# Carrying the softmax normalisation of five attention units through DRAM instead of TensorE

## The chip, the cores and the metric

The kernel runs on one core of one Trainium2 chip. The metric is the device time of one execution in microseconds (us); lower is better. The core has a matrix engine (TensorE, "PE" in the rows), a vector engine (VectorE, "DVE"), an activation engine (ScalarE, "ACT"), GpSimd ("POOL") and SyncE ("SP"), which here only starts DMA transfers. Each engine works through its own list of instructions in order. Between engines, an instruction waits on semaphores that others raise.

## The reference

Three stages follow one another. Only the first matters for the change.

```python
def _attn_ref(q, k, v):                       # batch 2, 8 heads, 576 positions, head size 64
    scores = scale * np.matmul(q, k.transpose(0, 1, 3, 2))
    ...                                       # bias by distance, window of 128 keys, causal
    attn = np.exp(scores - np.max(scores, axis=-1, keepdims=True))
    attn = attn / (np.sum(attn, axis=-1, keepdims=True) + 1e-09)
    return np.matmul(attn, v)

def reference(**kwargs):
    x = _attn_ref(...)                        # 1152 tokens x 512
    x = _moe_ref(x, ...)                      # 4 experts, 512 -> 1024 -> 512, relu, weighted sum
    return _moe2_ref(x, ...)                  # 512 -> 2048, h*cos(h), -> 512
```

## The kernel before, in words

**Attention.** The queries are cut into nine units of 128 columns. They are worked in the order `units = [1, 2, 3, 4, 0, 5, 6, 7, 8]`; this text numbers the nine by their place, 0 to 8, so place 4 is unit 0 (the first 64 queries of both batches, with 64 keys each). A unit has eight heads, done as two groups of four, so the list `sched` has 18 entries, and the loop in `attention` has a step k for each, two steps to a unit. The entries of place i are 2i and 2i+1.

In step k the program writes these pieces in this order (each engine takes its own parts of them in the same order):

- `att_transpose` of entry k-2: TensorE turns the probabilities into a PSUM tile `t_ps` (L525); VectorE (L531) and ScalarE (L532) copy half each into `pt`.
- `att_scores` of entry k: TensorE makes scores (`s_ps`, L443/L448/L455); VectorE adds the bias and takes the extreme, four instructions a step (L468, "reductions" below); ScalarE takes the exponentials and their sums into `dens` (L474).
- `att_factors` of entry k-2, if it is the second of its unit: TensorE turns the broadcast reciprocal sums `wide` into a PSUM tile `r_ps`, four transposes (L499), and ScalarE copies them to `rs` (L503).
- `att_sums` of entry k-1, likewise: VectorE adds the sums and takes reciprocals (L486, L489), GpSimd broadcasts them to `wide` (L491).
- `fill(k)`: one piece of weight preparation on GpSimd, sometimes a product of the next stage on TensorE (`fills`: steps 12, 13, 15, 16), and then `stage()`, which advances the generators that normalise finished units.
- `att_pv` of entry k-3 up to step 9 and of entry k-2 from step 9 on (step 9 does both): TensorE multiplies by the values into the PSUM tile `x_ps` (L546/L561).

When both entries of a unit are through `att_pv`, a generator `rest()` is queued. Its first advance runs `normal`, the VectorE product of `x_ps` and `rs` (L571), which is also the last read of `x_ps` for places 0 to 4. Then ScalarE and VectorE split the result into two parts (`own_early`, L355 and L190), or `transform_early` makes sums of two units.

**PSUM.** `x_ps` tiles come from a pool of two banks in turn, so the tile of place i+2 uses the bank of place i, and its first `att_pv` cannot start until the `normal` of place i has read that bank.

**Loads.** At the top of each even step, SyncE starts the loads of the unit two places ahead (`qt`, `kt`) and of the values `vt` of the unit at work.

**After attention** (from about 65 us on) come the two feed-forward stages: large products on TensorE, 128x512 each.

Of the kernel before, what the change touches and what calls it, by code (L numbers as in the profile page):

```python
# [10 lines left out]
F32 = mybir.dt.float32  # L11
# [5 lines left out]
ALU = mybir.AluOpType  # L17
# [3 lines left out]
B, H, S, D = 2, 8, 576, 64  # L21
# [9 lines left out]
NP = NB // 128  # L31
ND = DM // 128
# [20 lines left out]
def tile_kernel(ctx, tc, qT, kT, v, probs, w_1, w_2, w_in, w_out, out):  # L53
    nc = tc.nc
# [3 lines left out]
    dram = pool("dram", bufs=1, space=DRAM)  # L58
# [18 lines left out]
    mkp = ap("mkp", bufs=1)  # L77
# [4 lines left out]
    stp = ap("stp", bufs=6)  # L82
# [279 lines left out]
    def own_early(t, x1):  # L362

        hi, lo = parts(t)
        hi(B11, x1[:, 0:2])
        hi(B21, x1[:, 2:4])
        lo(B21, x1[:, 2:4], nc.gpsimd)
        yield
        lo(B11, x1[:, 0:2], nc.vector)
# [52 lines left out]
    state, xps = {}, {}  # L422

    dens = mkp.tile([128, 2, H, 2], F32, name="dens")

    def att_scores(u, g):
        i = place(u)[1] if u else 0
# [51 lines left out]

    recs, late = {}, {}  # L480

    def att_sums(u, g):
        if g == 0:
            return
        rec = stp.tile([128, H], F32, name="rec", tag="rec")
        nc.vector.tensor_reduce(  # L486
            out=rec, in_=dens[:, units.index(u) % 2], axis=mybir.AxisListType.X, op=ALU.add
        )
        nc.vector.reciprocal(out=rec, in_=rec)  # L489
        wide = recs[u] = stp.tile([128, H, D], F32, name="wide", tag="wide", bufs=1)  # L490
        nc.gpsimd.tensor_copy(wide, rec.unsqueeze(2).to_broadcast([128, H, D]))  # L491

    def att_factors(u, g):
        if g == 0:
            return
        rec = recs.pop(u)
        rt = ps1.tile([128, ND, 128], F32, name="r_ps", tag="o_ps")
        for d in range(ND):
            nc.tensor.transpose(  # L499
                rt[:, d, :], rec[:, 2 * d : 2 * d + 2].rearrange("p h d -> p (h d)"), ident  # L500
            )
        rs = stp.tile([128, ND, 128], F32, name="rs", tag="rs", bufs=2)
        nc.scalar.activation(out=rs, in_=rt, func=AF.Copy)  # L503
        recs[u] = rs
# [30 lines left out]
    def att_pv(u, g):  # L535
# [3 lines left out]
        xt = xps[u]  # L539
# [27 lines left out]
        if g == 1:  # L567

            def normal(out):
                rs = recs.pop(u)  # L570
                nc.vector.tensor_tensor(out=out, in0=xt, in1=rs, op=ALU.mult)  # L571

            def rest():
                if u == 0:
                    x1 = txp.tile([128, ND, 128], F32, name="x1", tag="x1", bufs=1)
                    normal(x1)
                    split(x0, x1, nc.gpsimd)
                    return
                t = (u - 1) % NP
                x1 = xk[:, :, t * 128 : (t + 1) * 128]  # L580
                if u <= NP:
                    normal(x1)
                    yield from own_early(t, x1)
                else:
                    normal(xt)
                    late[u] = transform_early(t, x1, xt, u == units[-1])
                    one, two, three, second, four, five = late[u]
                    if u >= units[-2]:
                        return
                    one()  # L590
                    two()
                    yield
                    if u < units[-3]:
                        for piece in (three, second, four, five):
                            piece()

            xps.pop(u)
            staged.append(rest())
# [5 lines left out]
    def load_units_to(k):  # L604
        while nloaded[0] < min(k, len(units)):
            load_unit(units[nloaded[0]])
            nloaded[0] += 1

    def attention(fill, finale):
        n = len(sched)  # L610
        at = lambda k, what: what(*sched[k]) if 0 <= k < n else None
        for k in range(n):
            if k % 2 == 0:

                load_units_to(k // 2 + 3)
                load_values(sched[k][0])
            at(k - LAG, att_transpose)
            at(k, att_scores)
            if k == n - 1:
                break  # L620
            at(k - LAG, att_factors)
            at(k - 1, att_sums)
            fill(k)
            if k <= CATCH:
                at(k - LAG - 1, att_pv)
            if k >= CATCH:
                at(k - LAG, att_pv)
        finale(n, at)
# [471 lines left out]
    def whole(step):  # L1100
        for _ in step:
            pass
# [115 lines left out]
    with tc.manual_schedule():  # L1218

        warm = probs_t[2][:, 0, :256]  # L1220
        nc.vector.memset(warm, 0.0)
        nc.vector.memset(dens, 1e-9)
        for _ in range(WARM):
            nc.tensor.matmul(  # L1224
                ps1.tile([128, 512], F32, name="o_ps", tag="o_ps")[:, :256],
                warm[:, :128], warm, start=True, stop=True,
            )
        load_units_to(2)
        constants()
        early = {}  # L1230
# [3 lines left out]
        def opening(j, kind):  # L1234
            early[j] = pair(0, j, kind)
            return early[j]

        def leftover(end):
# [2 lines left out]
            return half(first[0], end)  # L1241

        fills = {
            12: lambda: opening(0, 3), 13: lambda: early[0],
            15: lambda: leftover(False), 16: lambda: leftover(True),
        }

# [144 lines left out]
```

## Time and profile before

| | |
|---|---|
| median of 3 runs | 621.19 us (621.17 to 621.64) |
| profiled execution: time | 622.03 us |
| profiled execution: span of the core | 620.0 us |
| TensorE busy | 613.9 us, 99% of the span |
| VectorE, ScalarE, GpSimd busy | 453.0, 321.5, 353.0 us |

The span is the time between the first and the last instruction of the profile; the execution's own time is 2.0 us longer. Busy time of TensorE is the union of its matmuls with modelled ends, so small gaps between short matmuls can hide in it; they are read from the starts of instructions instead.

### The profile page before, as it was taken

The page shows a single profiled execution, that of the slowest core. Times are in us where ns is not written, and L with a number is a line of the kernel's source. Part 1 is how long each engine was busy: PE and PEld are TensorE (multiplying, and loading weights), DVE is VectorE, ACT ScalarE, POOL GpSimd, SP SyncE. Part 2 cuts the span into 40 slices and gives each one's busy share as a digit, 9 for nine tenths or more (in the row PEclk, how much of TensorE's full clock was granted, in tenths as well). Part 3 has the DMA queues.
Part 4 walks back from the last instruction along what each step waited for, and adds up shares of the span by engine and source line. Part 5 has one row for each costly group of instructions (what it writes and reads, how often), then busy time and mean ns, then how long its engine had stood idle before and what let it go on. Part 6 is the DMA issues. An engine that isn't in the chain of part 4 may idle for free.

```text
span 620.0 us, 9378 instructions
## 1 busy us (share of the span) xinstructions
PE 613.9 (99%) x3348; PEld 503.4 (81%) x3348; DVE 453.0 (73%) x780; ACT 321.5 (52%) x674; POOL 353.0 (57%) x335
## 2 busy tenths in 40 slices
PE   8999999999999999999999999999999999999998
PEld 6777888888888888888888888888888888888886
DVE  6868899589789789699689655668664664664663
ACT  6988554444443453443443421455873773673660
POOL 4877586383383373473473471496569479379330
PEclk9999999999999999999999999999999999999999
DMA  9641236347447347337245227621102202202003
GB/s 261 169 148 46 85 132 197 76 136 213 127 130 237 108 124 243 109 109 246 71 135 171 67 82 211 183 68 36 34 2 68 69 1 68 69 0 69 17 1 135
DMA packets 51246, 69.05 MB, mean 111 GB/s; under 512 B 6912, under 2 KB 31488, under 8 KB 51200
## 3 DMA queue, kind: packets, MB, share of 16 engines
q1 hardware_dynamic: 50656, 68.06, 36.1%
q8 instruction: 26, 0.43, 0.3%
q10 hardware_dynamic: 544, 0.39, 0.2%
q14 instruction: 20, 0.16, 0.1%
HBM read 53.76 MB, written 14.68 MB: 110 GB/s over the span
## 4 chain that ended last, share of the span: by engine, by line
PE 94%; ACT 2%; DVE 2%; POOL 1%; issue 1%; ACTq 0%; POOLq 0%; DVEq 0%
PE o_ps L913 43%; PE o_ps L720 35%; PE o_ps L774 5%; PE o_ps L1027 4%; PE x_ps L561 2%; PE t_ps L525 1%; PE s_ps L455 1%; PE r_ps L499 1%; PE o_ps L1224 1%; PE o_ps L953 0%; ACT u L658 0%; ACT r L659 0%; POOL w1t L190 0%; DVE p L468 0%; ACT u L666 0%
## 5 line engine op out<-in xcount | busy, mean ns | idle before, releaser
L913 PE MATMUL o_ps<-w2t,hpair 128*128 128x512 f32 x1044 | 241.5, 389 | 0.0
L913 PEld LDWEIGHTS o_ps<-w2t,hpair 128*128 128x128 f32 x1044 | 195.7, 188 | 40.7
L720 PE MATMUL o_ps<-xs,w1t 128*128 128x512 f32 x720 | 168.8, 390 | 0.0
L720 PEld LDWEIGHTS o_ps<-xs,w1t 128*128 128x128 f32 x720 | 134.8, 188 | 28.6 <-issue 0.5
L190 POOL TENSOR_TENSOR w2t<-raw,w2t 128x512 fp32r<-128x512 f32 x48 | 63.4, 1337 | 73.6 <-ACT w2t L214 73.4
L190 POOL TENSOR_TENSOR w1t<-raw,w1t 128x512 fp32r<-128x512 f32 x48 | 64.4, 1358 | 62.0 <-ACT w1t L214 61.6
L190 POOL TENSOR_TENSOR w1t<-sm,w1t 128x512 fp32r<-128x512 f32 x48 | 63.8, 1346 | 31.3 <-ACT w1t L214 31.0
L190 POOL TENSOR_TENSOR hpair<-u,hpair 128x512 fp32r<-128x512 f32 x30 | 40.2, 1346 | 52.4 <-ACT hpair L678 52.4
L720 PE MATMUL o_ps<-xz,w1t 128*128 128x512 f32 x288 | 69.8, 390 | 0.1
L313 ACT ACTIVATE cr<-cr 128x512 f32<-128x512 f32 x32 | 21.7, 679 | 81.7 <-DVE ca L307 81.7
L720 PEld LDWEIGHTS o_ps<-xz,w1t 128*128 128x128 f32 x288 | 53.8, 188 | 11.8 <-DVE c L822 0.7
L697 DVE SCALAR_TENSOR_TENSOR hpair<-o_ps,hpair 128x512 fp32r<-128x512 f32 x47 | 32.3, 687 | 19.2 <-ACT hpair L706 19.2
L706 ACT ACTIVATE hpair<-o_ps 128x512 fp32r<-128x512 f32 x47 | 28.0, 596 | 33.7 <-DVE o_ps L822 33.6
L214 ACT ACTIVATE w1t<-sm 128x512 fp32r<-128x512 f32 x44 | 27.6, 630 | 32.5 <-POOL sm L190 32.3
L934 DVE SCALAR_TENSOR_TENSOR accpair<-o_ps,pr,accpair 128x512 f32<-128x512 f32 x48 | 34.8, 745 | 10.4 <-PE o_ps L913 10.4
L662 DVE SCALAR_TENSOR_TENSOR u<-r,u 128x512 f32<-128x512 f32 x36 | 28.1, 781 | 14.1 <-ACT r L659 14.1
L942 DVE TENSOR_TENSOR accpair<-o_ps,accpair 128x512 f32<-128x512 f32 x23 | 15.7, 689 | 27.7 <-PE o_ps L913 27.7
L774 PE MATMUL o_ps<-w1t,x 128*128 128x512 f32 x144 | 35.7, 391 | 0.0
L822 DVE TENSOR_TENSOR o_ps<-o_ps,u 128x512 f32<-128x512 f32 x48 | 33.1, 691 | 3.0 <-PE o_ps L720 2.8
L913 PE MATMUL o_ps<-w2t,h 128*128 128x512 f32 x144 | 34.8, 389 | 0.0
L316 DVE SCALAR_TENSOR_TENSOR co<-cr,ca 128x512 f32<-128x512 f32 x32 | 33.4, 1043 | 1.4 <-ACT cr L313 0.4
L474 ACT ACTIVATE p<-p,nmax 128x192 f32<-128x192 f32 (+1 forms) x72 | 31.0, 437 | 5.2 <-DVE nmax L468 5.1
(147 smaller groups left out, 894.1 us busy)
## 6 DMA issues: line engine op xcount, KB each, us to landing
raw<-w SPq DMA_DIRECT2D x32, 512.0 KB, 4.2
cr<-w_in SPq DMA_DIRECT2D x16, 512.0 KB, 4.4
cr<-w_out SPq DMA_DIRECT2D x16, 512.0 KB, 4.6
wi<-co SPq DMA_DIRECT2D x16, 256.0 KB, 3.4
wo<-co SPq DMA_DIRECT2D x16, 256.0 KB, 2.3
raw<-wi SPq DMA_DIRECT2D x8, 512.0 KB, 3.5
raw<-wo SPq DMA_DIRECT2D x8, 512.0 KB, 3.6
qt<-qT SPq DMA_DIRECT2D x8, 256.0 KB, 4.0
```

The source lines that it names most:

```text
L190: eng.tensor_tensor(out=out, in0=a, in1=b, op=ALU.subtract)
L214: nc.scalar.activation(out=out, in_=src, func=AF.Copy)
L316: nc.vector.scalar_tensor_tensor(out=fl(o), in0=fl(hw), scalar=TINY, in1=fl(a), op0=ALU.is_ge, op1=ALU.mult,)
L474: nc.scalar.activation(out=p[:, k], in_=p[:, k], func=AF.Exp, scale=-1.0, bias=nmax[:, k : k + 1], accum_out=den[:, k, 0:1],)
L662: nc.vector.scalar_tensor_tensor(out=u, in0=r, scalar=MAGIC, in1=u, op0=ALU.subtract, op1=ALU.subtract)
L697: nc.vector.scalar_tensor_tensor(out=out, in0=src, scalar=0.0, in1=hi.bitcast(F32), op0=ALU.max, op1=ALU.subtract)
L706: nc.scalar.activation(out=hi, in_=src, func=AF.Relu)
L720: nc.tensor.matmul(ps, w(a, k, m), operand_of_x(bb, b)[:, m], start=(start and m == 0 and (a, bb) == PASSES[0]), stop=(stop and m == 1 and ...
L774: nc.tensor.matmul(ps.rearrange("p (j f) -> p j f", j=2), x0[:, bb, d, :], w1[:, :, a, 0, d * 256 : (d + 1) * 256], start=(d == 0 and (a, ...
L822: add = lambda out, a, b: nc.vector.tensor_tensor(out=out, in0=a, in1=b, op=ALU.add)
L913: nc.tensor.matmul(ps, hidden(a, f, t), w_t[2, g, f // 2][:, bb, f % 2, :], start=(f == 0 and (a, bb) == PASSES[0]), stop=(f == NFG - 1 an ...
L934: nc.vector.scalar_tensor_tensor(out=o, in0=ps, scalar=s, in1=o, op0=ALU.mult, op1=ALU.add)
```

## The change

It concerns places 1 to 5 (units 2, 3, 4, 0, 5). For these the reciprocals are written in an order of even and odd heads into a 128x32 tile, VectorE transposes its 32x32 squares, SyncE stores the result (16 KB) to DRAM, and one step later two DMAs read it back with broadcasting into `rs` (64 partitions x 4 x 128 each). GpSimd's broadcast, TensorE's four transposes and ScalarE's copy are not issued for them. Their `normal` is one step later (two steps for unit 4, whose parts then all follow at once). The two products of `fills` at steps 12 and 13 are at 13 and 14, and the loads of even steps stand behind `att_factors` and `att_sums` instead of ahead of the transposes.

```diff
+    inverse = mkp.tile([128, 2, 2, 32], F32, name="inverse")
+    inverse32 = dram.tile([2, 128, 32], F32, name="inverse32")
...
+    def carried(u):
+        return 0 < units.index(u) < 6
+
     def att_sums(u, g):
         if g == 0:
+            return
+        if carried(u):
+            i = units.index(u) % 2
+            rec, sq = inverse[:, i, 0], inverse[:, i, 1]
+            nc.vector.tensor_reduce(
+                out=rec[:, :H].rearrange("p (e m) -> p m e", e=2),
+                in_=dens[:, i].rearrange("p (m e) t -> p m e t", e=2),
+                axis=mybir.AxisListType.X, op=ALU.add,
+            )
+            nc.vector.reciprocal(out=rec[:, :H], in_=rec[:, :H])
+            nc.vector.transpose(sq, rec)
+            nc.sync.dma_start(out=inverse32[i], in_=sq)
             return
...
     def att_factors(u, g):
         if g == 0:
+            return
+        if carried(u):
+            i = units.index(u) % 2
+            rs = stp.tile([128, 4, ND, 32], F32, name="rs", tag="rs", bufs=2)
+            src = inverse32[i].rearrange("(a c) j -> a (c j)", a=4)
+            for hh in range(2):
+                nc.sync.dma_start(
+                    out=rs[64 * hh : 64 * hh + 64].rearrange("p a m j -> p a (m j)"),
+                    in_=src[:, 128 * hh : 128 * hh + 128].unsqueeze(0).to_broadcast([64, 4, 128]),
+                )
+            recs[u] = rs
             return
...
             def rest():
+                if carried(u):
+                    yield
+                    if u == NP:
+                        yield
                 if u == 0:
...
                 if u <= NP:
                     normal(x1)
-                    yield from own_early(t, x1)
+                    parts_of = own_early(t, x1)
+                    if u == NP:
+                        whole(parts_of)
+                    yield from parts_of
...
+        def loads(k):
+            load_units_to(k // 2 + 3)
+            load_values(sched[k][0])
+
+        loads(0)
         for k in range(n):
-            if k % 2 == 0:
-
-                load_units_to(k // 2 + 3)
-                load_values(sched[k][0])
             at(k - LAG, att_transpose)
             at(k, att_scores)
             if k == n - 1:
                 break
             at(k - LAG, att_factors)
             at(k - 1, att_sums)
+            if k and k % 2 == 0:
+                loads(k)
             fill(k)
...
         fills = {
-            12: lambda: opening(0, 3), 13: lambda: early[0],
+            13: lambda: opening(0, 3), 14: lambda: early[0],
             15: lambda: leftover(False), 16: lambda: leftover(True),
         }
```

How the rows of each engine move is shown at three places.

TensorE, steps 10 and 11, before (`s_ps` scores, `x_ps` products with the values, `t_ps` transposes of the probabilities, `r_ps` of the reciprocals; brackets name the engines whose semaphores are waited for):

```order
L448 MATMUL s_ps<-kt,qt 128x192 x2
L546 MATMUL x_ps<-pt,v_200 64x64 [waits DVE_49]
L546 MATMUL x_ps<-pt,v_200 64x64
L546 MATMUL x_ps<-pt,v_200 64x64 [waits Activation_49]
L546 MATMUL x_ps<-pt,v_200 64x64 x5
L525 MATMUL t_ps<-ident,p_128 64x64 [waits PE_49]
L525 MATMUL t_ps<-ident,p_128 64x64 x7
L448 MATMUL s_ps<-kt,qt 128x192 [waits DVE_49] x2
L448 MATMUL s_ps<-kt,qt 128x192 x2
L499 MATMUL r_ps<-ident,wide 128x128 [waits Pool_49]
L499 MATMUL r_ps<-ident,wide 128x128 x3
L546 MATMUL x_ps<-pt,v_200 64x64 [waits DVE_49]
```

The same place with the change:

```order
L450 MATMUL s_ps<-kt,qt 128x192 x2
L574 MATMUL x_ps<-pt,v_203 64x64 [waits DVE_49]
L574 MATMUL x_ps<-pt,v_203 64x64
L574 MATMUL x_ps<-pt,v_203 64x64 [waits Activation_49]
L574 MATMUL x_ps<-pt,v_203 64x64 x5
L553 MATMUL t_ps<-ident,p_128 64x64 [waits PE_49]
L553 MATMUL t_ps<-ident,p_128 64x64 x7
L450 MATMUL s_ps<-kt,qt 128x192 x4
L574 MATMUL x_ps<-pt,v_203 64x64 [waits DVE_49]
```

The `r_ps` transposes are gone, and the scores of step 11 no longer wait for VectorE, though the reductions of step 10 must still have read the PSUM tile that they overwrite: the wait of the first `x_ps` product, ahead of them, already covers those reductions.

VectorE, step 10, before, from the fourth reduction on (`xs` is the split of a normalised unit, `xk<-x_ps,rs` is `normal`, here of place 3; that of place 2 is in step 9):

```order
L468 ISA p_129,nmax<-s_ps,bm_132 128x192
L468 ISA nmax 128x1
L486 TENSOR_REDUCE rec<-dens 128x8 [waits Activation_49]
L489 RECIPROCAL rec<-rec 128x8 [waits DVE_49]
L190 TENSOR_TENSOR xs<-xk,xs 128x2x128 [waits Activation_49]
L571 TENSOR_TENSOR xk<-x_ps,rs 128x4x128
L531 COPY pt<-t_ps 64x4x64 [waits PE_49]
```

With the change (here `normal` is that of place 2; place 3's follows in step 12):

```order
L470 ISA p_129,nmax<-s_ps,bm_132 128x192
L470 ISA nmax 128x1
L493 TENSOR_REDUCE inverse<-dens 128x4x2 [waits Activation_49]
L498 RECIPROCAL inverse<-inverse 128x8 [waits DVE_49]
L499 STREAM_TRANSPOSE inverse<-inverse 128x32 [waits DMAHW7_49,DVE_49]
L602 TENSOR_TENSOR xk<-x_ps,rs 128x4x128 [waits DMAHW4_49,DMAHW3_49]
L559 COPY pt<-t_ps 64x4x64 [waits PE_49]
```

`normal` of place 2 has moved behind the reductions and the sums of step 10, and now waits for two DMAs; place 4's first `att_pv`, which needs its bank, stands in step 10 on TensorE in both.

SyncE, steps 4 to 6, as a difference (`inverse_144` is the DRAM tile, `inverse` the tile on the core):

```order
+L500 DMA inverse_144<-inverse 128x32
 L148 DMA qt<-qT 128x512
 L151 DMA kh<-kT 128x4x64 x2
 L180 DMA vt<-v 128x512
-L1260 DMA pr<-probs 128x9x4
+L1303 DMA pr<-probs 128x9x4
+L518 DMA rs<-inverse_144 64x4x128 x2
+L500 DMA inverse_144<-inverse 128x32
 L165 DMA qt<-qT 128x512
 L168 DMA kt<-kT 128x4x192
 L180 DMA vt<-v 128x512
```

Each store stands ahead of the loads of its step, and each pair of reads ahead of the next store.

## Rows read from the trace of the kernel before

**Rows 1.** The page, part 1: busy time of each engine.

```profile
PE 613.9 (99%) x3348; PEld 503.4 (81%) x3348; DVE 453.0 (73%) x780; ACT 321.5 (52%) x674; POOL 353.0 (57%) x335
```

**Rows 2.** Stretches: length, busy time of each engine, granted clock, DMA share, GB/s.

```profile
47.83:65.22 17.39, 17.39 (x244) 13.48 (x243) 15.40 (x55) 15.18 (x52) 13.43 (x17) 1.00 0.11 39
500.00:600.00 100.00, 100.00 (x446) 82.75 (x445) 59.23 (x86) 62.00 (x111) 64.06 (x57) 1.00 0.12 35
```

**Rows 3.** Timeline of TensorE, steps 5 to 14: start, length, line, [idle before].

```profile
18.05 0.66 PE L499 MATMUL r_ps<-ident,wide 128*128 128x128 f32 x4
18.63 1.09 PE L561 MATMUL x_ps<-pt,vt 128*64 128x128 f32 x16
19.66 0.71 PE L525 MATMUL t_ps<-ident,p 64*128 64x64 f32 x16
...
27.25 1.07 PE L525 MATMUL t_ps<-ident,p 64*128 64x64 f32 x16
...
31.55 0.87 PE L448 MATMUL s_ps<-kt,qt 64*128 64x192 f32 x8
32.35 0.89 PE L546 MATMUL x_ps<-pt,v 64*64 64x64 f32 x16
...
33.43 1.19 PE L448 MATMUL s_ps<-kt,qt 64*128 64x192 f32 x8
34.78 0.66 PE L499 MATMUL r_ps<-ident,wide 128*128 128x128 f32 x4 [0.16 <-POOL wide L491]
...
35.94 0.57 PE L546 MATMUL x_ps<-pt,v 64*64 64x64 f32 x12 [0.24 <-ACT pt L532]
...
37.84 1.66 PE L720 MATMUL o_ps<-xs,w1t 128*128 128x512 f32 x6
39.43 0.65 PE L561 MATMUL x_ps<-pt,v 64*64 64x128 f32 x8
...
42.01 0.66 PE L499 MATMUL r_ps<-ident,wide 128*128 128x128 f32 x4
42.42 1.63 PE L720 MATMUL o_ps<-xs,w1t 128*128 128x512 f32 x6
...
45.80 0.88 PE L455 MATMUL s_ps<-kt,qt 64*64 64x192 f32 x16
46.81 1.09 PE L561 MATMUL x_ps<-pt,vt 128*64 128x128 f32 x16
```

**Rows 4.** Timeline of VectorE, from steps 4, 8 and 10.

```profile
17.00 0.20 DVE L489 RECIPROCAL rec<-rec 128x8 f32<-128x8 f32 x1
...
26.62 0.21 DVE L468 CUSTOM_DVE_ANT_0 p<-s_ps,bm 128x64 f32<-128x64 f32 x1
...
32.45 0.36 DVE L468 CUSTOM_DVE_ANT_0 p<-s_ps,bm 128x192 f32<-128x192 f32 x1 [0.22 <-PE s_ps L448]
...
33.57 0.17 DVE L486 TENSOR_REDUCE rec<-dens 128x8 f32<-128x16 f32 x1
33.77 0.20 DVE L489 RECIPROCAL rec<-rec 128x8 f32<-128x8 f32 x1
33.89 0.37 DVE L190 TENSOR_TENSOR xs<-xk,xs 128x256 fp32r<-128x256 f32 x1
34.18 0.68 DVE L571 TENSOR_TENSOR xk<-x_ps,rs 128x512 f32<-128x512 f32 x1
```

**Rows 5.** Line 785, VectorE's transposes of 32x32 squares: ns min/median/max, starts.

```profile
L785 DVE STREAM_TRANSPOSE lt<-o_ps x7: 703/708/718, 95.8 to 372.4; 128x512 f32<-128x512 f32 x7
```

**Rows 6.** Tile `vt`, the loads of values: us from issue to landing.

```profile
DMA to landing us min/median/max: 3.9/4.6/7.8
```

**Rows 7.** Tile `lm`, four reads of 64 KB from DRAM each time: issue to landing.

```profile
DMA to landing us min/median/max: 1.8/4.0/6.7
```

**Rows 8.** SyncE's DMA queue: the first load of step 4, the values of step 4.

```profile
12.16 0.34 SPq L148 DMA_DIRECT2D qt<-qT  x1
13.61 2.61 SPq L180 DMA_DIRECT2D vt<-v  x1
```

More of the change, by code (lines that the diff above doesn't have):

```diff
@@ L569, in normal @@
             def normal(out):
-                rs = recs.pop(u)
-                nc.vector.tensor_tensor(out=out, in0=xt, in1=rs, op=ALU.mult)
+                rs, x = recs.pop(u), xt
+                if carried(u):
+                    rs = rs.rearrange("p a m j -> p m a j")
+                    out, x = (t.rearrange("p m (a j) -> p m a j", j=32) for t in (out, xt))
+                nc.vector.tensor_tensor(out=out, in0=x, in1=rs, op=ALU.mult)
             def rest():
+                if carried(u):
+                    yield
+                    if u == NP:
+                        yield
                 if u == 0:
@@ L1222, in tile_kernel @@
         nc.vector.memset(dens, 1e-9)
+        nc.vector.memset(inverse[:, :, 0], 0.0)
         for _ in range(WARM):
```

## The prediction

> **What bounds the kernel now.** I read the page first: TensorE is busy 99% of the span, the other engines 52 to 73% [rows 1]. The table by stretches then says where that matters: from 47.83 us to the end of attention, and in the feed-forward stages, TensorE is busy all the time at a granted clock of 1.00 [rows 2]. So nothing later can hide a delay of TensorE, and nothing later gives one back: what the change does to the start of TensorE's work behind attention it does to the whole time. That leaves the stretch it edits, steps 4 to 15, some 14 to 50 us. There I went through TensorE's timeline by starts, since the busy share counts modelled ends: the place of every start shows what the engine spent on the group before it [rows 3]. VectorE's timeline in the same stretch gives the length of the chain that the moved `normal` stands in [rows 4].
>
> I write S, V, T and R for a step's scores, products with the values, transposes of the probabilities and transposes of the reciprocals.
>
> **What it removes.** R is gone for five places, in steps 5, 7, 9, 11 and 13. The first takes TensorE from 18.05 to 18.63, 0.58 us; the next three are alike; the last takes 0.41, from 42.01 to 42.42, the product behind it starting earlier [rows 3]. Together 4 x 0.58 + 0.41 = **2.73 us** saved, if TensorE is what everything else waits for. ScalarE loses five copies and GpSimd five broadcasts; neither is priced by itself, since their worth is the waits of TensorE that they cause. Those show as groups that take longer than their like: T in step 9 takes 1.07 where the one at 19.66 takes 0.71 (0.36); S in step 11 lasts from 33.43 to 34.78 where that of step 10 takes 31.55 to 32.35 (1.35 less 0.80: 0.55, the 0.16 before R in it); V in step 11 waits 0.24 for ScalarE; S in step 14 lasts from 45.80 to 46.81 (1.01 less 0.80: 0.21) [rows 3]. All are waits for engines that are relieved, or fall where TensorE comes later anyway: **1.36 us** saved, between 0 (all come back) and 1.36.
>
> **What it moves: `normal`, and with it two waits.** The PSUM bank is what I trace. Place i+2's first V writes the bank that `normal` of place i reads. Before, `normal` of place 2 is in step 9 and that of place 3 in step 10, so V of step 10 (32.35) and of step 12 (39.43) find their banks free: the one starts as S ends, the other as the product between them ends [rows 3]. With the change `normal` of place 2 is in step 10 and of place 3 in step 12, the very steps whose V needs the bank, and on VectorE it stands behind that step's reductions and sums. The reductions need that step's S. So between S and V a serial chain appears, whatever head start the engines have:
>
> - end of S to the first reduction: 0.10 (32.35 to 32.45);
> - four reductions: 1.12 (32.45 to 33.57);
> - sum 0.20 (33.57 to 33.77), reciprocal 0.20, then the new transpose of 128x32, which must wait for it [rows 4]. The trace has no transpose of that size: one of 128x512 takes 0.71 [rows 5], a sum of 8 columns 0.17 [rows 4]. These are its bounds; I take 0.15, next to the small one, for it is a sixteenth of the large. Together 0.55;
> - `normal` 0.68 [rows 4], taken as unchanged (same elements; its second operand is read in runs of 32), and 0.10 to TensorE.
>
> That is **2.55 us** in step 10. TensorE has no other work queued between S and V there, and behind V stand T, S and V of step 11. In step 12 the same chain holds. Before, a product stood between S and V (37.84 to 39.43, 1.59 us [rows 3]) and would have covered most of it; it has moved to step 13. VectorE has besides two copies and the split of place 2 ahead of its reductions, so I take **2.60**. The product itself costs nothing by being moved: the same six matmuls run a step later. After step 12 `normal` runs a step ahead of the V that needs its bank.
>
> **Smaller terms.** Place 1's `normal` is now in step 8, a step ahead of the V that needs its bank, but VectorE comes to it late: the copy, four short reductions (0.21 each, overlapping), 0.55, 0.68 [rows 4] are about 2.3 us behind S of step 8, and TensorE has V, T and a short S, about 2.1 us, to do in between. With a copy on ScalarE behind it I take 0.30, between 0 and 0.6. The three new VectorE transposes off that path, and the stores' issue, lie beside other work.
>
> At the end, unit 5's last four VectorE half-tile operations move from step 15 to step 16, where unit 6's `normal` already stands; at 0.37 each (the split of 33.89 [rows 4]) that is 1.5 us ahead of the copy that step 17's V needs. VectorE is idle 2.0 of the 17.39 us of that stretch [rows 2]. I take 0.40, between 0 and 1.5.
>
> **Transfers.** Loads of even steps now stand behind the store, which waits for VectorE. Step 4's first load left at 12.16 and its values at 13.61 [rows 8]; the reciprocal that the store follows is done at 17.20 [rows 4], so the values leave at about 19.1. They take 3.9 to 7.8 [rows 6], landing from 23.0 on; the V of step 7 that reads them comes, by two steps of some 2.5 us (T of steps 6 and 9 are 7.6 apart) behind 18.63 [rows 3], near 23.5. The queue then holds less than it did, so I take the lower end and no cost; the upper end would cost 3.5. The broadcast reads of 256 KB are nearest to the reads of `lm`, 1.8 to 6.7 us [rows 7]. They are issued near 21 for a `normal` near 26.7; only the upper end is late, by about 1. Later places have more room. Price in the sum: 0.
>
> **Sum.** -2.73 - 1.36 + 2.55 + 2.60 + 0.30 + 0.40 = **+1.8 us**. Against the profiled execution (622.03 us, span 620.0) that makes 623.8; its time is 0.84 above the median, so the median is predicted at 621.2 + 1.8 = **623.0 us**, +0.28%. A measurement here can tell about 0.2%, 1.24 us, from no change.
>
> **Rivals.**
>
> *Faster.* The new waits may be short, if TensorE comes to V late for another cause or VectorE early. For it: the work taken off TensorE and its old waits are worth 4.1 us together. Against it: the reductions of step 10 cannot start before S of step 10 ends, and the order of VectorE puts them ahead of `normal`; even with a free VectorE the chain is 2.4 us. It decides once the two waits together fall below 3.4 us (4.1 less the smaller terms), against 5.15. With half of the waits the time is 620.4, with none 617.8; I put it at 619.5.
>
> *Transfers late.* The values of place 2 or 3 land with 5 to 8 us instead of 4, or the reads of place 1 at the upper end. For it: the loads start some 5 us later than before, right behind each other, and the reads are many short runs. Against it: the queue is emptied of the very loads that moved. A delay before step 10 comes on top, since it shifts S and with it the whole chain: 1 to 3.5 us more, 625.
>
> *The clock falls.* All rows here stand at 1.00, the higher of two levels, 2.4 GHz [rows 2], and the longest pause of TensorE in these rows is 0.24 [rows 3]; a pause of 2.55 us is not in them. If the clock went to 1.2 GHz behind each of the two, the next step's 2.5 us would take 5.0, together 5 more: 628. The Trainium skill, page "TensorE: Matmul & The Clock Gate", section "Part 1: The HAM clock gate", has such a rule: an idle TensorE is put back to half its clock and gets it again only after sustained work. By that rule it hangs on whether these waits count as idle; no run here shows it.
>
> *Nothing measurable.* Not a mechanism of its own but the low end of the forecast: a shorter transpose, no cost at steps 9 and 17, 1.0 us or a little less.
>
> **How the numbers follow.** Forecast 0.70 (of which 0.22 within 1.24 us), faster 0.10, late transfers 0.13, clock 0.07. The likeliest case alone spans 622.0 (smaller terms at 0) to 624.4 (a transpose of 0.4 in both waits, old waits partly kept). The range for all, leaving out most of the faster case, half of the late transfers and the clock: 621.4 to 624.8. Faster by over 0.2%: 0.10; within: 0.23; slower: 0.67.
>
> **What would show it.** In the profile after, TensorE's R matmuls fall from 36 to 16. Right: V of step 10 (line 574) and V of step 12 (line 589) start about 2.5 us after their S ended, with VectorE's line 602 as releaser; T of step 9 is back at 0.7; TensorE's starts are about 1 us ahead of before up to step 9 and 1 to 2 us behind from step 13 on. Wrong: V in those steps close behind S; waits of V for a DMA, or of `normal` for one; a granted clock below 1.00 between 30 and 45 us; or a lag at step 15 that is gone by 100 us.

## The result, and the profile after

The kernel with the change takes 628.98 us (median of 4 runs, 628.21 to 630.59), the kernel before 621.23 (621.17 to 621.64): ratio 1.0127, 95% interval 1.0105 to 1.0148. The forecast was 623.0, range 621.4 to 624.8: the direction is right, the size is not, and the time lies outside the range. The profiled run took 628.5 us with a span of 626.7, 6.7 more than before.

The page of the kernel after, busy time and the granted clock in 40 equal slices (against [rows 1]):

```profile
PE 613.2 (98%) x3328; PEld 502.5 (80%) x3328; DVE 454.8 (73%) x786; ACT 320.3 (51%) x669; POOL 350.9 (56%) x330
...
PEclk9969999999999999999999999999999999999999
```

TensorE has the 20 matmuls less that were announced. New is the 6 in the third slice (31 to 47 us). The table by stretches, with the columns of [rows 2], shows it closer:

```profile
26.00:34.00 8.00, 5.45 (x108) 4.30 (x98) 7.76 (x40) 6.69 (x29) 4.63 (x6) 1.00 0.66 195
34.00:46.00 12.00, 9.35 (x125) 7.10 (x128) 6.58 (x28) 6.73 (x26) 6.16 (x8) 0.57 0.76 205
46.00:60.00 14.00, 14.00 (x178) 10.20 (x171) 8.93 (x40) 10.81 (x37) 6.32 (x7) 1.00 0.30 94
```

For 12 us the mean granted clock is 0.57: TensorE is mostly at the lower of its two levels, 1.2 GHz. TensorE's timeline of the same kernel, the rows that answer to [rows 3], and step 17:

```profile
17.33 1.09 PE L589 MATMUL x_ps<-pt,vt 128*64 128x128 f32 x16
...
22.30 0.44 PE L589 MATMUL x_ps<-pt,vt 128*64 128x128 f32 x4
24.24 0.88 PE L589 MATMUL x_ps<-pt,vt 128*64 128x128 f32 x12 [1.50 <-DMA vt<-v]
...
25.69 0.46 PE L445 MATMUL s_ps<-kh,qt 64*64 64x64 f32 x16
26.08 1.09 PE L589 MATMUL x_ps<-pt,vt 128*64 128x128 f32 x16
27.11 0.72 PE L553 MATMUL t_ps<-ident,p 64*128 64x64 f32 x16
27.75 0.46 PE L445 MATMUL s_ps<-kh,qt 64*64 64x64 f32 x16
28.32 2.33 PE L589 MATMUL x_ps<-pt,vt 128*64 128x128 f32 x32
...
30.84 0.87 PE L450 MATMUL s_ps<-kt,qt 64*128 64x192 f32 x8
34.13 0.68 PE L574 MATMUL x_ps<-pt,v 64*64 64x64 f32 x16 [2.43 <-DVE xk L602]
...
34.99 0.92 PE L450 MATMUL s_ps<-kt,qt 64*128 64x192 f32 x8
35.84 1.12 PE L574 MATMUL x_ps<-pt,v 64*64 64x64 f32 x16
36.89 1.06 PE L553 MATMUL t_ps<-ident,p 64*64 64x64 f32 x16
37.88 1.56 PE L457 MATMUL s_ps<-kt,qt 64*64 64x192 f32 x16
41.96 1.11 PE L589 MATMUL x_ps<-pt,v 64*64 64x128 f32 x8 [2.52 <-DVE xk L602]
43.00 1.12 PE L589 MATMUL x_ps<-pt,vt 128*64 128x128 f32 x8
44.05 1.06 PE L553 MATMUL t_ps<-ident,p 64*64 64x64 f32 x16
45.04 1.29 PE L457 MATMUL s_ps<-kt,qt 64*64 64x192 f32 x16
46.26 1.66 PE L762 MATMUL o_ps<-xs,w1t 128*128 128x512 f32 x6
...
52.06 1.09 PE L589 MATMUL x_ps<-pt,vt 128*64 128x128 f32 x16
...
62.05 1.09 PE L589 MATMUL x_ps<-pt,vt 128*64 128x128 f32 x16 [1.40 <-DVE xz L190]
```

Four waits stand in it: for values in step 7, for `normal` in steps 10 and 12, for the half-tile work of unit 5 in step 17. Groups between 35.8 and 46.3 take up to 1.8 times their usual time. T of step 12 takes 1.06; in the kernel before it took 0.66:

```profile
36.44 0.66 PE L525 MATMUL t_ps<-ident,p 64*64 64x64 f32 x16
```

VectorE's timeline at step 10 shows the chain behind the first `normal` wait, from the first reduction through sum, reciprocal and the new transpose to `normal` of place 2:

```profile
31.74 0.36 DVE L470 CUSTOM_DVE_ANT_0 p<-s_ps,bm 128x192 f32<-128x192 f32 x1
...
32.85 0.17 DVE L493 TENSOR_REDUCE inverse<-dens 128x8 f32<-128x16 f32 x1
33.05 0.20 DVE L498 RECIPROCAL inverse<-inverse 128x8 f32<-128x8 f32 x1
33.29 0.21 DVE L499 STREAM_TRANSPOSE inverse<-inverse 128x32 f32<-128x32 f32 x1
33.43 0.65 DVE L602 TENSOR_TENSOR xk<-x_ps,rs 128x512 f32<-128x512 f32 x1
```

SyncE's queue in steps 4 and 5 (against [rows 8]), and below it a row of the chain that ended last, the landing of the values loaded at 18.66:

```profile
16.77 0.34 SPq L500 DMA_DIRECT2D inverse<-inverse  x1
...
18.66 0.50 SPq L180 DMA_DIRECT2D vt<-v  x1
...
19.74 2.00 SPq L518 DMA_DIRECT2D rs<-inverse  x2
```

```profile
18.66 5.53 DMA vt<-v
```

The values land at 24.19; TensorE wanted them at 22.74. From V of step 5 (18.63 before [rows 3], 17.33 after) to V of step 14 (46.81 and 52.06) TensorE needs 28.18 us before and 34.73 after, 6.55 more. The terms, with R saved in steps 7, 9, 11 and 13 only: -2.15 for R, -1.36 for old waits, +2.43 and +2.52, +1.50 for the values, +0.18 at step 9, and +3.27 for the groups from 34.99 to 46.26 at low clock: 6.39. (The 3.27, each group against the same one of e14 at clock 1.00, by starts and for S of step 12 by length: S 0.85 less 0.80, V 1.05 less 0.61, T 0.99 less 0.60, S 1.56 less 0.88, V 2.09 less 1.18, T 0.99 less 0.60, S 1.22 less 0.81.) Step 17 adds 1.40 behind that. Ahead of it stands a lead: V of step 5 starts 1.30 us sooner than before, of which its R is 0.58. The other 0.72 is in no term; e1, e5 and e7, whose programs are the same up to step 9, start this V between 17.04 and 17.99, so it can be the spread of single executions. Together 6.55 + 1.40 - 1.30 = 6.65, the lag at the end of attention.

### The profile page after: what moved, and what is told of

It is laid out like the page before. It is cut to its first block, busy times and chain, and to the rows that moved or that the text cites. A ratio compares the mean times of both kernels' runs of the same rounds, so it can differ in the third digit from the quotient of the medians.

```text
span 626.7 us, 9354 instructions
## 1 busy us (share of the span) xinstructions
PE 613.2 (98%) x3328; PEld 502.5 (80%) x3328; DVE 454.8 (73%) x786; ACT 320.3 (51%) x669; POOL 350.9 (56%) x330
## 4 chain that ended last, share of the span: by engine, by line
PE 92%; DVE 3%; ACT 3%; DMA 1%; issue 1%; SPq 0%; DVEq 0%; ACTq 0%
PE o_ps L955 43%; PE o_ps L762 34%; PE o_ps L816 5%; PE o_ps L1069 3%; PE x_ps L589 2%; PE t_ps L553 1%; PE s_ps L457 1%; DMA vt<-v 1%; DVE p L470 1%; PE o_ps L1267 1%; ACT p L476 1%; PE o_ps L995 0%; ACT u L700 0%; ACT r L701 0%; PE r_ps L527 0%
## 5 line engine op out<-in xcount | busy, mean ns | idle before, releaser
L739 DVE SCALAR_TENSOR_TENSOR hpair<-o_ps,hpair 128x512 fp32r<-128x512 f32 x47 | 32.3, 688 | 19.2 <-ACT hpair L748 19.1
```

Source lines behind the costliest of these rows:

```text
L739: nc.vector.scalar_tensor_tensor(out=out, in0=src, scalar=0.0, in1=hi.bitcast(F32), op0=ALU.max, op1=ALU.subtract)
```

## The experiments

Each time stands beside runs of the kernel before on the same chip (medians 621.28 to 621.88). The changed kernel itself was not run again on those chips, so a difference from its 628.98 is good to some 0.6 us.

**e1_filler.** Eight matmuls on the identity, whose result nobody reads, stand between S and V of steps 10 and 12.

```diff
             at(k, att_scores)
+            if k in (10, 12):
+                idle = ps1.tile([128, 512], F32, name="o_ps", tag="o_ps")
+                for _ in range(8):
+                    nc.tensor.matmul(idle[:, :128], ident, ident, start=True, stop=True)
```

> The changed kernel with eight dummy 128x128 matmuls on TensorE between scores and products with the values in steps 10 and 12 (their result is not used; everything else is computed). Theory: the two waits of 2.4 and 2.5 us let the granted clock fall, and the matmuls from 34 to 46 us, at the lower clock, cost about 3.1 us. Keeping the engine at work in the waits should keep the clock at 1.00 in that stretch and bring the median from 629.0 to about 626 us, although work is added; the waits themselves stay near 2.5 us from end of scores to V. Rival, the slow matmuls have another cause (their operands): the time stays at 629 or rises by what of the filler sticks out.

625.29 us, ratio 1.0066 (1.0050 to 1.0083). TensorE's timeline at step 10, and the stretch that stood at 0.57:

```profile
31.35 2.05 PE L662 MATMUL o_ps<-ident 128*128 128x128 f32 x16
33.85 0.68 PE L574 MATMUL x_ps<-pt,v 64*64 64x64 f32 x16 [0.45 <-DVE xk L602]
```

```profile
34.00:46.00 12.00, 11.12 (x168) 8.64 (x168) 8.16 (x36) 8.87 (x35) 6.19 (x8) 1.00 0.78 220
```

V comes no sooner for the filler, which only fills the pause; the clock stays at 1.00, and 3.7 us come back by the medians. Between the two profiled runs the stretch from V of step 5 to V of step 14 is 2.80 shorter (17.04 to 48.97). So the price of the low clock is 2.8 to 3.7 us, with the 3.27 read from the groups in between.

**e2_loads_first.** The loads stand at the top of each even step again.

```diff
         for k in range(n):
+            if k % 2 == 0:
+                loads(k)
...
-            if k and k % 2 == 0:
-                loads(k)
```

> The changed kernel with the loads of even steps back at the top of the step. Theory: only the wait of TensorE for the values of place 2 in step 7 (1.5 us in the profile) goes; the waits for VectorE in steps 10 and 12 and the lower clock stay: about 627.5 us. Rival, transfers cause most of the loss: 623 to 624 us. If the reads back now come later because the loads stand ahead of the store, VectorE's line that normalises would show a wait, and the gain is smaller than 1.5 us.

631.32 us, ratio 1.0155 (1.0133 to 1.0178): worse. The wait of step 7 is gone, but in step 9 TensorE waits 1.29 us for the next values and in step 10 it waits 3.21 for `normal`. On SyncE the reads wait for their store to land, which has loads ahead of it, and the next loads wait behind the reads: those of step 5 start at 21.65, 3.81 behind their store (17.84), the loads of step 6 at 23.02. SyncE's row in its table of waits between 14 and 48 us (waited for, total, times, longest):

```profile
SPq L518 <- DMA inverse<-inverse: 15.1, 4, 4.7
```

**e3_normal_back.** Each `normal` is in its old step, the products at 12 and 13; only the way through DRAM is left.

```diff
-                if carried(u):
-                    yield
-                    if u == NP:
-                        yield
...
-                    if u == NP:
-                        whole(parts_of)
...
-            13: lambda: opening(0, 3), 14: lambda: early[0],
+            12: lambda: opening(0, 3), 13: lambda: early[0],
```

> The changed kernel with the normalisation of the five places and the two products back at their steps of before; the reciprocals still go through DRAM and the loads still come late. Theory: the waits for the banks in steps 10 and 12, the low clock and the wait in step 17 go, worth 2.4 + 2.5 + 3.1 + 1.4 = 9.4 us together; the wait for the values of place 2 (1.5 us) stays: about 620 us. Rival, the delay was needed: the normalisation then waits on VectorE for the reads, in the order of 2 us for each place and everything queued behind it, and the time stays above 625 us.

626.24 us, ratio 1.0075 (1.0060 to 1.0090). Two rows of VectorE in its table of waits between 14 and 50 us show why the change has the later `normal` at all: without it VectorE stands still until the reads land.

```profile
DVE x L602 <- DMA rs<-inverse: 4.0, 1, 4.0
DVE xk L602 <- DMA rs<-inverse: 3.0, 2, 2.4
```

Its clock does not go by the length of one pause. It falls between 38 and 42 us, behind a pause of TensorE of 1.40 us in step 11 with three of about 0.4 near it, and stays at 1.00 behind one of 2.21 us in step 13:

```profile
46.82 1.62 PE L756 MATMUL o_ps<-xs,w1t 128*128 128x512 f32 x6 [2.21 <-ACT p L864]
```

```profile
38.00:42.00 4.00, 4.00 (x30) 2.45 (x26) 2.44 (x13) 3.08 (x14) 2.96 (x4) 0.58 0.98 276
...
46.00:50.00 4.00, 3.18 (x36) 2.33 (x38) 1.29 (x9) 3.44 (x13) 2.67 (x3) 1.00 0.48 150
```

**e4_only_late.** The kernel before, with only the later normalisation and the products at 13 and 14; R stays on TensorE, and there are no transfers.

```diff
             def rest():
+                if 0 < units.index(u) < 6:
+                    yield
+                    if u == NP:
+                        yield
```

> The kernel before with only the later normalisation of five places and the two products a step later; reciprocals as before through TensorE, loads as before. Theory: the waits in steps 10 and 12, the low clock behind them and the wait in step 17 appear here without any of the new transfers: about 621 + 5 + 3 + 1 = 630 us, less some waits of before that are absorbed, 628 to 631. Rival, the transfers cause the loss: within 2 us of 621.

629.65 us, ratio 1.0126 (1.0109 to 1.0143): the whole loss, without any of the new transfers. Step 17 waits 1.40 here too. Its rows for V of steps 10 and 12, and its table by stretches:

```profile
34.47 1.12 PE L546 MATMUL x_ps<-pt,v 64*64 64x64 f32 x16 [2.16 <-DVE xk L571]
...
44.37 1.12 PE L561 MATMUL x_ps<-pt,v 64*64 64x128 f32 x8 [2.26 <-DVE xk L571]
```

```profile
34.00:48.00 14.00, 11.28 (x124) 8.58 (x128) 6.49 (x27) 7.40 (x30) 9.06 (x12) 0.52 0.35 112
```

**e5_place5_back.** Unit 5 is normalised in its old step, nothing else is changed.

```diff
-                if carried(u):
+                if carried(u) and u != 5:
                     yield
```

> Unit 5 (place 5) normalises in its old step again; everything else is as changed. Theory: VectorE's half-tile operations of unit 5 leave step 16, the 1.4 us wait of TensorE's V in step 17 goes, and the time falls from 629.0 to about 627.6. Rival: V of step 17 is late for another reason (the split of unit 6 itself, or the copies of T), the wait stays and so does the time, 629.0.

628.43 us, ratio 1.0117 (1.0097 to 1.0137). The wait of step 17 is gone, as the theory has it, but the wait for values in step 7 is 2.51 in the profiled run, and single runs spread from 627.3 to 631.4: the 1.4 us can't be seen in the time.

**e6_values_first.** The values are loaded first in each even step.

```diff
         def loads(k):
+            if k:
+                load_values(sched[k][0])
             load_units_to(k // 2 + 3)
-            load_values(sched[k][0])
+            if not k:
+                load_values(sched[k][0])
```

> In each even step after the first the values are loaded ahead of the queries and keys; everything else is as changed. Theory: the values of step 7 leave SyncE 1.5 to 2 us sooner, TensorE's wait for them (1.50 us in step 7) goes, the rest of the loss stays: about 627.5. Rival: the 1.5 us were only in front of later waits that end at a time of their own (VectorE's chain in step 10), or the queries and keys are now late instead: 629.0 or more.

631.09 us, ratio 1.0168 (1.0149 to 1.0187). The wait for values is gone, and S of step 10 waits 1.25 us for its keys instead: the rival.

**e7_normal_ahead.** `normal` of places 2 and 3 stands ahead of the reductions of steps 10 and 12.

```diff
+            if k in (10, 12):
+                stage()
             at(k - LAG, att_transpose)
...
-            stage()
+            if k not in (10, 12):
+                stage()
```

> VectorE's normal of places 2 and 3 stands ahead of the reductions of steps 10 and 12 and not behind them; nothing else is changed. Theory: no serial chain between S and V is left, so the waits of 2.43 and 2.52 us go, and with them the low clock between 34 and 46 us (3.1 us): 629.0 - 8.05 = about 621, granted clock 1.00 in all stretches. If the clock fell for another reason (the transfers), the waits go but not the 3.1 us: 624. Rival: normal needs the delay, because its reads through DRAM land late; VectorE then waits for a DMA in step 10 or 12, as it did with the normalisation in its old place: 625 to 627.

628.08 us, ratio 1.0108 (1.0094 to 1.0122), where 621 was expected; the interval overlaps that of the changed kernel, so a gain is not shown. Both waits for `normal` are gone, but others have grown; two rows of TensorE's timeline and the stretches behind them:

```profile
24.55 0.88 PE L589 MATMUL x_ps<-pt,vt 128*64 128x128 f32 x12 [1.75 <-DMA vt<-v]
...
41.58 0.66 PE L589 MATMUL x_ps<-pt,vt 128*64 128x128 f32 x8 [1.87 <-DMA vt<-v]
```

```profile
26.00:30.00 4.00, 4.00 (x74) 3.30 (x72) 2.71 (x14) 3.04 (x12) 0.89 (x2) 0.63 0.85 260
...
42.00:46.00 4.00, 4.00 (x41) 2.74 (x37) 2.35 (x11) 1.84 (x7) 0.09 (x1) 0.58 0.98 248
```

The wait in step 7 stands ahead of the edit; it differs from run to run (0.96 in e1, 1.50 after, 2.51 in e5). In step 12 values are late that leave SyncE at 36.89 and take 4.6; in the changed kernel they left at 34.86, took 4.9 and were there before the chain on VectorE was through. Ahead of that wait TensorE waits 1.21 for a copy of ScalarE. The clock falls behind both places.

**e8_all_mended.** The three diffs above together, and the products back at 12 and 13 (the last lines of e3's diff).

> The three edits above together, and the two products back at steps 12 and 13. Theory: what is left of the change is the work it takes off TensorE and the old waits for the relieved engines (-2.73 - 1.36 us), so 621.2 - 4.1 = 617.1, with 1 to 2 us of small waits 618 to 619: faster than before. Rival: the reads through DRAM cost a wait of their own somewhere once nothing else is late, and the time is that of before or above, 621 or more.

625.58 us, ratio 1.0066 (1.0054 to 1.0079). Keys are late in step 10 (1.33 us), copies of VectorE and ScalarE behind them (0.74 and 0.36), and the clock is 0.50 from 34 to 38 us.

**e9_other_queue, e10_all_other_queue, e11_act_queue.** The store and the reads are started by GpSimd, the loads stand at the top of even steps (e2's diff). The second has the edits of e7 and e5 besides, with the products back; the third is the second with `nc.scalar` in the place of `nc.gpsimd`.

```diff
-            nc.sync.dma_start(out=inverse32[i], in_=sq)
+            nc.gpsimd.dma_start(out=inverse32[i], in_=sq)
...
-                nc.sync.dma_start(
+                nc.gpsimd.dma_start(
                     out=rs[64 * hh : 64 * hh + 64].rearrange("p a m j -> p a (m j)"),
```

> The store and the two reads of each place are started from GpSimd's queue, and the loads stand at the top of each even step, as before the change; VectorE's order is as changed. Theory: on SyncE the reads wait in order for their store to land and hold up the loads behind them; on another queue they hold up none, so TensorE waits nowhere for values. What is left is -2.73 - 1.36 for the work and waits removed, 2.43 + 2.52 for normal in steps 10 and 12, about 3.1 for the low clock behind these and 1.4 in step 17: 621.2 + 5.4 = 626.6. Rival: the values are late because the transfers share the DMA engines, not because of the queue; then TensorE still waits 1 to 3 us for vt or kt and the time stays near 629.

> As the run before, and normal of places 2 and 3 ahead of the reductions of steps 10 and 12, unit 5 in its old step, the products back at steps 12 and 13. Theory: neither the chain on VectorE nor the queue holds TensorE up, the clock stays at 1.00, and the work removed shows: 621.2 - 4.1 = 617.1, at most 619. Rival: the reads land too late for normal even so, or GpSimd's held-up weight preparation comes late: 621 or more.

> As the run before, with the store and the reads started from ScalarE's queue and not from GpSimd's. Theory: ScalarE now waits in order for the store to land, 1.4 to 5 us each time, and its exponentials and copies behind it are late: TensorE waits for ScalarE's copies, 2 to 8 us above the run before, 620 to 627. Rival: the store lands within the step between, ScalarE does not wait, and the time is that of the run before.

630.60, 631.39 and 629.58 us; ratios 1.0149 (1.0135 to 1.0163), 1.0163 (1.0149 to 1.0177) and 1.0131 (1.0118 to 1.0145). In the first two no load is late, as the theory has it, but GpSimd comes to the store behind its weight preparation, waits for the store to land ahead of the reads of place 2 (1.62 and 1.83 us), and `normal` of place 2 waits for these reads, 1.10 and 4.14 us. VectorE's row in step 10 of the second:

```profile
33.50 0.69 DVE L602 TENSOR_TENSOR xk<-x_ps,rs 128x512 f32<-128x512 f32 x1 [4.14 <-DMA rs<-inverse]
```

In the third TensorE waits 2.72 us for a copy of ScalarE in step 7: the store of place 1 leaves at 16.40 and lands after 4.4, and only then ScalarE starts the reads (20.82), which take it 1.32 to issue. So reads that wait for their store held up what stood behind them in the queue of each of the three engines (of SyncE in e2). The Trainium skill, page "DMA: Bandwidth & Descriptors", section "Issuing engines are not separate DMA queues", says that DMAs started by different engines run on the same 16 DMA engines and interleave, so that another issuing engine saves only the time of issuing. No run here shows it by itself: the reads land after 3.4, 3.6 and 4.3 us (medians) in these three and after 4.9 in the changed kernel, with the loads in another order.

**e12_loads_early.** The edits of e7 and e5, products back, all transfers on SyncE, and the loads of an even step started in the step before, ahead of the reads.

```diff
             at(k, att_scores)
...
+            if k % 2 == 1:
+                loads(k + 1)
             at(k - LAG, att_factors)
             at(k - 1, att_sums)
-            if k and k % 2 == 0:
-                loads(k)
```

> Normal of places 2 and 3 ahead of the reductions of steps 10 and 12, unit 5 in its old step, products back at 12 and 13; the transfers stay on SyncE, but the loads of an even step are started in the step before it, behind its scores and ahead of the reads through DRAM. Theory: the reads' wait for their store then holds up no load that is needed soon; TensorE waits for no transfer, the clock stays at 1.00, and 621.2 - 4.1 = 617.1, at most 619.5. Rival: the bytes themselves are the cost (all 16 DMA engines are busy), a load or a read is late whatever the order: 622 to 625, the clock below 1.00 in some stretch.

625.43 us, ratio 1.0057 (1.0040 to 1.0074). TensorE waits for no load at all. What is left is mainly the way through DRAM itself (and 1.12 us for a copy of ScalarE in step 14). SyncE's store and reads of place 2, and VectorE's `normal` of place 2 in step 10:

```profile
23.49 0.55 SPq L500 DMA_DIRECT2D inverse<-inverse  x1
...
26.96 2.04 SPq L518 DMA_DIRECT2D rs<-inverse  x2
```

```profile
32.22 0.69 DVE L602 TENSOR_TENSOR xk<-x_ps,rs 128x512 f32<-128x512 f32 x1 [1.48 <-DMA rs<-inverse]
```

Its store leaves SyncE at 23.49, its reads start at 26.96 and are issued by 29.00, the product starts at 32.22: 8.7 us, and steps 8 and 9, the short ones of unit 0, stand in that time. V of step 10 then waits 2.33 us, and the clock is 0.54 from 34 to 38.

**e13_transfers_alone.** The kernel before, with the transpose, the stores and the reads added in the change's order on SyncE, read into a tile that is written again later; R and `normal` as before.

```diff
         nc.vector.reciprocal(out=rec, in_=rec)
+        if carried(u):
+            nc.vector.transpose(inverse[:, i, 1], inverse[:, i, 0])
+            nc.sync.dma_start(out=inverse32[i], in_=inverse[:, i, 1])
...
+            spare = acc0[:, :].rearrange("p (a m j) -> p a m j", a=4, j=32)
```

> The kernel before, with the square's transpose, the stores and the reads added on SyncE in the order of the change (the loads behind the store too), but read into a tile that nobody uses: normalisation, its transposes on TensorE and the order of VectorE's other work are as before. Theory of two causes: the values are late by 1 to 3 us in steps 7 to 9, the clock may fall behind that wait, 623 to 626. The prediction's price of 0 for the transfers: 621.3 to 621.8 (five short transposes on VectorE at most).

623.82 us against 621.88, ratio 1.0035 (1.0022 to 1.0048): the transfers, with the five transposes and the later loads that belong to them, cost about 2 us. The values of step 7 are in time here. One row of it, step 9:

```profile
30.50 1.75 PE L582 MATMUL x_ps<-pt,vt 128*64 128x128 f32 x28 [0.61 <-DMA vt<-v]
```

The rest is spread over waits of 0.2 to 0.4 for GpSimd's broadcast and ScalarE; no pause is over 0.61, and the clock stays at 1.00.

**e14_three_places.** e12 with places 1, 3 and 5 alone through DRAM, and `normal` ahead in step 12 only.

```diff
     def carried(u):
-        return 0 < units.index(u) < 6
+        return units.index(u) in (1, 3, 5)
```

> Only places 1, 3 and 5 go through DRAM; places 2 and 4 are normalised as before the change. Place 3's normal stands ahead of the reductions of step 12, unit 5 is in its old step, the products are at 12 and 13, and the loads of an even step start in the step before, ahead of the reads. Theory: in the run with all five and these edits what was left was place 2's normal waiting for its reads (2.3 us at V of step 10, and the low clock behind it) and GpSimd late with place 4 (1.1 us); with both gone the two or three transposes saved show: 0.58 x 2 + 0.41 = 1.6 us, and about half of the old waits, 0.7, so 621.9 - 2.3 = 619.6, 621 at most. Rival: the bytes of the reads still delay a load or a read somewhere: 621.9 to 624.

622.25 us (11 runs) against 621.68, ratio 1.0007 (0.9998 to 1.0015): no difference that can be told. V of step 10 waits 0.76 for VectorE's copy and 0.36 for ScalarE's, the first product 0.54 and 0.33 for the split of place 3. From V of step 5 to V of step 14 it needs 28.81 us (17.92 to 46.73) where before needs 28.18, with the clock at 1.00 throughout. V of step 5 comes 0.71 us sooner than before, V of step 14 only 0.08: short waits take back the R saved in steps 5, 9 and 13.

**e15_late_but_ahead.** e4 with `normal` ahead of the reductions in steps 10 and 12, unit 5 in its old step.

> The kernel before with the later normalisation alone (no transfers, R on TensorE as before, the products at 13 and 14), but normal of places 2 and 3 ahead of the reductions of steps 10 and 12, and unit 5 in its old step. Theory: the loss of 8 us that the later normalisation made by itself is the chain reductions, sums, normal between S and V, and the low clock behind it; without the chain it is gone, 621.9, at most 622.9. Rival: a later normalisation costs by being later (GpSimd's and ScalarE's parts, the products): 624 or more.

624.77 us, ratio 1.0049 (1.0034 to 1.0064), so 5.3 of e4's 8.4 us are gone (1.4 of them the wait of step 17), not all: VectorE's copy of the probabilities, behind `normal` and the reductions, is late in step 12, where no product covers it any more:

```profile
39.51 0.65 PE L561 MATMUL x_ps<-pt,v 64*64 64x128 f32 x8 [1.97 <-DVE pt L531]
```

The clock is 0.71 from 42 to 46. The rival has a part in it.

## Why the prediction was wrong

**What bounds the kernel: right.** The first product behind attention starts at 71.88 us, before at 65.22: 6.66 later, and the span is 6.7 longer. Nothing later gives anything back.

**What it removes: right.** R is gone; T of step 9 takes 0.72 where it took 1.07, S of step 11 0.85 to the next start where it took 1.35. The 4.1 us fit into the sums of the first section; the 0.24 of V in step 11 can't be read by itself, since that group ran at the low clock. e14 shows what the condition (TensorE is what everything else waits for) is worth: with three R gone and the clock at 1.00 throughout, TensorE was 0.08 us ahead in step 14.

**The two waits for `normal`: right, in place, releaser and size.** 2.43 and 2.52 us against 2.55 and 2.60; the transpose took 0.21 (0.15 assumed), `normal` 0.65. e7 shows by taking them away that they are VectorE's order, e4 that they need no transfer.

**Steps 8 and 9: right in sign.** V of step 9 starts 0.57 behind S, whose like in step 8 takes 0.39 (and in e3, with `normal` in its old step, 0.39 too): 0.18 against 0.30. V of step 9 itself lasts 2.26 us to the next start where it took 1.90 before; these 0.36 were in no term, and the rows do not name what it waits for.

**Step 17: mis-sized.** 1.40 against 0.40. All four half-tile operations and `normal` of unit 6 stand ahead of what V needs; the upper end, 1.5, was the price. The idle 2.0 us of VectorE that argued for less lie elsewhere. e5 takes the wait away.

**Transfers: the step that priced them at 0 failed.** The values left at 18.66 (19.1 predicted), 5.05 later than before, and took 5.53, where the lower end of 3.9 to 7.8 was taken because the queue held less; and TensorE, being ahead, wanted them at 22.74 and not near 23.5. That is the 1.50 us in step 7. The queue holds more than was counted, the store and 256 KB of reads in short runs, but whether these slow the values is not shown: in the kernel before the same values took 7.5, from 13.61. e13 measures the transfers at about 2 us, without any later normalisation.

**The clock: the step that priced a pause at its length alone failed, and it is the largest miss.** The rival put at 0.07 is what happened: 3.3 us by the groups, 3.7 by e1. The forecast had the clock in its sum at nothing, since no row of before had a pause over 0.24. What that rival worked out, 628, is within 0.2% of the measurement, but in part by luck: it took 5 for the clock, and left out the 1.50 for the values and 1.0 of step 17. The Trainium skill, page "TensorE: Matmul & The Clock Gate", section "Part 1: The HAM clock gate", has the clock halved for an idle engine and given back after sustained work; the granted clock of 0.57 behind pauses of 2.43 and 2.52 us agrees in direction.

With the measured terms the forecast's own sum is -2.73 - 1.36 + 2.43 + 2.52 + 0.18 + 1.40 + 1.50 + 3.27 = 7.2 us, against 7.75 of the medians and 6.5 of the two profiled runs. The lead of 0.72 us at V of step 5, which the sum does not have, is the difference from the latter.

**What the sum hid.** Terms in a row do not come off one by one. The later normalisation (with the products a step later) costs 8.4 us by itself, the transfers 1.9, both 7.7, though that kernel also saves R. e7 removed two waits of 5 us together and gained 0.9 by the medians, no clear gain, because others grew, and the clock fell behind these as it had behind the old ones. The mendings together (e8, e12) gain 3.4 to 3.6 and no more: the way through DRAM takes 8.7 us in the hurried place, and on TensorE R took 0.58. No version tried is faster than the kernel before. How the 2 us of e13 divide between the order on SyncE and the bytes is left open: no run had the transfers alone in another order.

## What to carry to other kernels

A new pause of a busy TensorE may have to be priced twice, as its length and as what follows at half clock (about 3 us here behind two pauses of 2.4 to 2.5, nothing behind one of 2.21 in e3); a few matmuls without use in the pause tell the two apart. When an instruction that waits (a store for VectorE, a read for its store) is put on an in-order DMA queue, the loads behind it are late too, and the lower end of their landing times is not to be taken without a row that shows it. Before a small job is taken from a busy engine, compare its length there (0.58 us) with the latency of the way around (8.7), and look for the consumer that is in a hurry.

## What the runs showed of the hardware

- The clock fell behind pauses in which TensorE did nothing for 1.75 (e7), 1.97 (e15), 2.33 (e12) and 2.43 us (after), to a mean of 0.50 to 0.71 in a stretch of 4 us within the next 8; after single pauses of 1.50 and 1.40 us (after) it stayed at 1.00, and with matmuls of no use in the pause too (e1). The length of a pause does not settle it: the clock stayed at 1.00 behind 2.21 us (e3, step 13), and fell behind several short ones in a row (1.40 with three of about 0.4 in e3; 1.33, 0.74 and 0.36 in e8).
- In the kernel after it came back at about 46 us, some 12 us behind the first pause, the second pause lying between.
- A transpose of 128x32 on VectorE took 0.21 us; one of 128x512 takes 0.71 [rows 5].
- A broadcast read of 128 KB took 0.59 to 0.99 us to issue and 3.5 to 6.0 to land in the kernel after; a store of 16 KB landed after 1.4 us in the kernel after (median) and after 4.6 where loads were ahead of it (e2, median).
